# Value loads of the first head pair on two hardware queues, and another order for batch 1's attention

## The chip, the cores and the metric

The kernel runs on one core of a Trainium2 chip. The metric is the device time of one execution in microseconds (us), the median of three runs. The core has five engines that run side by side, each with its own list of instructions in order: TensorE (PE, matrix products; its weight loads appear as PEld), VectorE (DVE), ScalarE (ACT), GpSimd (POOL) and SyncE (SP). Sixteen DMA engines move data between HBM and the on-chip memory. A transfer is issued from SP or ACT (the hardware queues) or from POOL (the software queue, the one that here casts f32 to bf16 on the way).

## The reference

```python
# q, k, v: (8 batches, 8 heads, 1024 positions, 64), f32; E, F: (64, 1024)
k_proj = np.einsum('ks,bhsd->bhkd', E, k)
v_proj = np.einsum('ks,bhsd->bhkd', F, v)
scores = scale * np.matmul(q, k_proj.transpose(0, 1, 3, 2))
attn = softmax(scores)                       # with + 1e-09 in the denominator
x = np.matmul(attn, v_proj)                  # -> (8192 tokens, 512)
...
h = x @ w_in                                 # (512, 2048)
g = h * np.clip(h + 3.0, 0.0, 6.0) / 6.0
out = g @ w_out                              # (2048, 512) -> (8192, 512)
```

The softmax is written out in the reference; it is shortened here to its name.

## The kernel before

The work goes by batch. A batch has 1024 tokens in two blocks of 512 (t = 0, 1). For each block the second half of the program, the two large products, runs 16 groups of `w_in` (a group `fo` gives 128 of the 2048 columns: four 128x512 matmuls over the four parts `ko` of the model's width, L424, then a Relu on ACT, L429, and a product on DVE, L430) and 4 groups of `w_out` (16 matmuls each, L444, then a copy to `o_sb`, L458, and a store from SP, L459). The `w_out` groups of one block are put between the `w_in` groups of the next.

The attention of a batch is worked out ahead and put between these groups. `Attention.project` (L181, 16 matmuls) reduces keys and values with E and F; `keys_out` and `values_out` copy the results on DVE; `turn` transposes the keys with a DMA, and issues later batches' loads on POOL. Heads are taken in four pairs (index j, head pairs 2j and 2j+1). For pair j, `scores` (L209) makes two banks, `exps` (L218) turns them into `aT` on ACT, `sums` and `values` (both L227) make two banks each, `log` and `inverse` (L159, L163) give 1/sum as exp(-ln) on ACT, and `scaled` (L246) writes `xT[:, j]` on DVE, which the `w_in` groups of the next batch read at `ko` = j. The on-chip accumulators are 8 banks, four in the pool `mm` and four in `at`.

Order on every engine is the order of the program text (`manual_schedule`); nothing reorders it. Generators let one function's matmuls be interrupted by others': `second_group` yields after every four of its 16 matmuls.

Batch 0 and batch 1 have their own code:

- At the start, SP loads E and ACT loads F into `ef_f32`. POOL issues, in this order, k and half of q for the pairs 0 to 3, v for the pairs 0 to 3 (L101, `load_pair`), seven pieces of `w_in`, the other half of q, `w_out`, and batch 1's k, v and q. POOL has eight semaphores for its loads, so that each load's issue waits for the landing of the eighth before it. `First.first_block` runs batch 0's first block pair by pair: `keys` (L296), `queries` (L324), `scores`, `keys_transposed`, and then `vals(j)` (L312) for the four pairs between `sums` and `products`. The `vals` of pair 3 is its last reduction.
- `two_groups` runs the first two `w_in` groups of a block together, `ko` by `ko`, so that the last part of `xT` is wanted later. It is used at the head of batch 0's two blocks, and (L545 to L548) at the head of the first block of batches 1 and 2.
- Batch 1's attention: after the group `fo` = 7 of batch 0's second block comes `project`, with `turn` and the two `values_out` in the gaps behind `fo` = 8, 9 and 10. Its four `visit` calls come in the four `w_out` groups of that block, each after the group's first four matmuls: visit 0 makes the scores of three pairs (six banks), visit 1 sums and values of pair 0 and scores of pair 3, visit 2 sums and values of pair 1 and sums of pair 2, visit 3 values of pair 2, sums and values of pair 3. Banks of both pools are used.
- Batches 2 to 7 use the same four visits, in later places. Batch 2's last visit comes directly ahead of batch 2's first `w_in` group; the others have a block in between.

Of the kernel before, what the change touches and what calls it, by code (L numbers as in the profile page):

```python
# [8 lines left out]
f32 = mybir.dt.float32  # L9
# [6 lines left out]
def kernel(  # L16
# [11 lines left out]
    nc = tc.nc  # L28
# [5 lines left out]
    P = 128  # L34
    SO = S // P
    KO = d_model // P
    FO = d_ff // P
    TOK = 512
    NB = S // TOK
    SB = SO // NB  # L40
# [17 lines left out]
    rpool = ctx.enter_context(tc.tile_pool(name="r", bufs=4))  # L58
# [13 lines left out]
    ef_f32 = consts.tile([P, S], f32, name="ef_f32")  # L72
    nc.sync.dma_start(out=ef_f32[:KP], in_=E)
    nc.scalar.dma_start(out=ef_f32[KP:], in_=F)
    nc.scalar.preload_act_table_set("natural_log_exp_and_others")
    ones = consts.tile([P, TOK], bf16, name="ones")
    nc.vector.memset(ones, 1.0)  # L77
# [14 lines left out]
    kqv = {0: {n: raw_tile(n) for n in ("k", "q", "v")}}  # L92
# [6 lines left out]
    def load_pair(n, j):  # L99
        hs = slice(2 * j, 2 * j + 2)  # L100
        nc.gpsimd.dma_start(out=kqv[0][n][:, hs], in_=kqv_dram[n][0][:, hs])  # L101

    for j in range(KO):
        load_pair("k", j)
        load_q0(0, slice(2 * j, 2 * j + 2))
        if j == 0:
            make_identity(nc, ident)
    for j in range(KO):
        load_pair("v", j)

    def load_kqv(b, order="qkv"):
        kqv[b] = {}
# [13 lines left out]
    for i in range(SB):  # L126
        c = slice(i * FO // SB, (i + 1) * FO // SB)
# [20 lines left out]
    def q_transposed(b):  # L148

        t = qT_pool.tile([P, KO, 2, TOK], bf16, tag="qT", name="qT")  # L150
        nc.sync.dma_start_transpose(t.rearrange("p j a (m n) -> p (j a m) n", n=P),
                                    kqv[b]["q"].rearrange("p h s d -> p (h s d)"))
        return t
# [14 lines left out]
    class Attention:  # L168
# [82 lines left out]
        def visit(self, n, following, later):  # L251
            if n == 0:
                last = self.scores(2, pmm)
                firsts = [self.scores(j, pat) for j in range(2)]
                for j, tiles in zip((2, 0, 1), (last, *firsts)):
                    self.exps(j, tiles)
                return lambda: None
            if n == 1:
                den, av = self.sums(0, pmm, pmm), self.values(0, pat, pat)
                last = self.scores(3, pat)  # L260
                recs = self.inverses(den)
                self.exps(3, last)
                return lambda: self.scaled(0, av, recs)
            if n == 2:
                den, av = self.sums(1, pmm, pmm), self.values(1, pat, pat)
                more = self.sums(2, pat, pat)
                recs = self.inverses(den)
                self.recs = []
                later += [lambda i=i: self.recs.append(log(more[i])) for i in range(NB)]
                later += [lambda i=i: inverse(self.recs[i]) for i in range(NB)]  # L270
                return lambda: self.scaled(1, av, recs)
            early = self.values(2, pmm, pmm)
            den, av = self.sums(3, pmm, pat), self.values(3, pat, pat)
            if following:
                following.project()
            self.scaled(2, early, self.recs)
            recs = self.inverses(den)
            if following:
                following.keys_out()
                later += [following.turn] + [lambda a=a: following.values_out(a) for a in range(2)]  # L280
            return lambda: self.scaled(3, av, recs)

# [142 lines left out]
    def h_out(h_ps, g, fo):  # L427
        r = rpool.tile([P, TOK], f32, tag="r", name="r")
        nc.scalar.activation(r, h_ps, AF.Relu, bias=0.5, scale=1.0 / 6.0)  # L429
        nc.vector.scalar_tensor_tensor(g[:, fo, :], r, 1.0, h_ps, op0=ALU.min, op1=ALU.mult)  # L430

    def first_group(xT, t, g, fo):
        h_ps = pmm()
        h_part(h_ps, xT, t, fo, range(KO))
        h_out(h_ps, g, fo)
# [5 lines left out]
    def second_group(b, t, g, c, copy=None):  # L441
        o_ps = pmm()
        for fo in range(FO):
            nc.tensor.matmul(o_ps, g[:, fo, c * P:(c + 1) * P], w_out_sb[:, fo, :],  # L444
                             start=(fo == 0), stop=(fo == FO - 1))
            if fo % SB == SB - 1:
                yield
        o_sb = opool.tile([P, d_model], f32, tag="o_sb", name="o_sb")
        o_dst = out_rows(b, t, c)
        if (b, t, c) == (B - 1, NB - 1, SB - 1):  # L450

            half = slice(0, d_model // 2), slice(d_model // 2, d_model)
            nc.vector.tensor_copy(o_sb[:, half[0]], o_ps[:, half[0]])
            nc.scalar.copy(o_sb[:, half[1]], o_ps[:, half[1]])
            nc.sync.dma_start(out=o_dst[:, half[0]], in_=o_sb[:, half[0]])
            nc.scalar.dma_start(out=o_dst[:, half[1]], in_=o_sb[:, half[1]])
            return
        (copy or nc.scalar.copy)(o_sb, o_ps)  # L458
        nc.sync.dma_start(out=o_dst, in_=o_sb)  # L459

    def whole(gen):
        for _ in gen:
            pass
# [13 lines left out]
    g = [g_tile(), g_tile()]  # L477


    def two_groups(xT, t, g, kos, more=lambda: None):  # L480
        tiles = [pmm(), pmm()]
        for i, (fo, part) in enumerate([(fo, part) for part in kos for fo in range(2)]):
            h_part(tiles[fo], xT, t, fo, part)
            if i == 0:
                more()
        for fo in range(2):
            h_out(tiles[fo], g, fo)

    two_groups(xT, 0, g[0], ((0, 1), (2,), (3,)), lambda: next(by_pairs, None))
    for fo in range(2, FO):  # L490
        first_group(xT, 0, g[0], fo)
        if fo >= FO - 2:
            first.queries(1, (0, 1) if fo == FO - 2 else (2, 3))
    behind, later = [], []
    second = Attention(1)
    second.xT = x_next

    def pop():
        if later:
            later.pop(0)()  # L500

    rows = [second_group(0, 0, g[0], c) for c in range(SB)]
    for i in range(SB + 1):
        for c in range(SB - 1):
# [2 lines left out]
            first.second_scores()  # L507
        elif i < 3:
            first.second_values(2 * i - 2)
    two_groups(xT, 1, g[1], ((0, 1), (2, 3)))  # L510
    for fo in range(2, FO):
        first_group(xT, 1, g[1], fo)
        pop()
        if fo == 7:
            second.project()
            second.keys_out()
            later += [second.turn, *(lambda a=a: second.values_out(a) for a in range(2))]
        elif fo == 11:
            whole(rows[3])
    rest = []  # L520
    for c in range(SB):
        for i, _ in enumerate(second_group(0, 1, g[1], c, nc.vector.tensor_copy)):
            pop()
            if i == 0:
                rest.append(second.visit(c, None, later))
            elif i == 2 or c == SB - 1:
                while rest:
                    rest.pop()()
    qT_dma[2] = q_transposed(2)
    xT = x_next  # L530

    second = Attention(2)
    for b in range(1, B):
        if b + 1 < B:
            x_next = second.xT = x_tile()
        third = Attention(b + 2) if b + 2 < B else None
        n = 0
        for t in range(NB):  # L540
            if b == 1 and t == 1:
                qT_dma[3] = q_transposed(3)
            g = g_tile()
            for fo in range(FO):
                if b < 3 and t == 0 and fo < 2:  # L545

                    if fo == 0:
                        two_groups(xT, t, g, ((0, 1, 2), (3,)))  # L548
                else:
                    first_group(xT, t, g, fo)  # L550
                pop()
                if b > 1 and t == 0 and fo == 5 and third:
                    qT_dma[b + 2] = q_transposed(b + 2)
                if b == 1 and t == 0 and fo == 10:
                    second.project()
                    second.keys_out()
                    later += [second.turn, *(lambda a=a: second.values_out(a) for a in range(2))]
                if not behind or fo % SB < SB - 1:
                    continue
                if b + 1 == B or n == 4:  # L560
                    whole(second_group(*behind[0], fo // SB))
                    continue
                rows = second_group(*behind[0], fo // SB, nc.vector.tensor_copy)
                if n < 3:
                    next(rows)
                    next(rows)
                    rest = second.visit(n, third, later)
                    whole(rows)
                else:
                    whole(rows)  # L570
                    rest = second.visit(n, third, later)
                rest()
                n += 1
            behind = [(b, t, g)]
        second, xT = third, x_next
# [32 lines left out]
```

## Time and profile before

| | us |
|---|---|
| median of 3 runs | 510.52 (510.51 to 510.60) |
| the profiled execution, its own time | 510.52 |
| its span from first to last instruction | 508.7 |
| PE busy | 497.5 |
| ACT busy | 274.0 |
| DVE busy | 258.0 |
| POOL busy | 37.9 |

Granted clock of TensorE: 1.000 over the whole span. In the groups of instructions, L444 is busy 231.6 us and L424 229.1 us, 379 ns each; since matmuls overlap in the pipeline, the distance between two starts says more than the duration. In the windows and timelines below, times count from the span's start; "idle before" is the time for which the engine had nothing to do, and the arrow names what ended it.

### The profile page before, as it was taken

What the parts mean: (1) busy time and instruction counts of PE and PEld (TensorE: products, weight loads), DVE (VectorE), ACT (ScalarE), POOL (GpSimd) and SP (SyncE); (2) the same over time, 40 slices, a digit from 0 to 9 for tenths busy, and PEclk for the clock granted to TensorE, in tenths of its full rate; (3) what the DMA queues carried; (4) which work ended last, traced back from release to release, by engine and by line L of the source; (5) the groups of instructions that cost most, each with busy time, mean ns of one, the idle gap of its engine ahead of it and who ended that gap; (6) DMA issues with size and microseconds to landing.
All of it is one profiled execution on the core that took longest, in us unless ns stands there. A gap on an engine that the chain in (4) does not pass through costs nothing.

```text
span 508.7 us, 7106 instructions
## 1 busy us (share of the span) xinstructions
PE 497.5 (98%) x2750; PEld 224.3 (44%) x2802; DVE 258.0 (51%) x401; ACT 274.0 (54%) x493; POOL 37.9 (7%) x57
## 2 busy tenths in 40 slices
PE   8899999999999999999999999999999999999996
PEld 4444444444444444444444444444444444444442
DVE  3572746856755733556444743467444563334420
ACT  3657476567475545664466644674447654444431
POOL 8610020010100200002000020000000000000000
PEclk9999999999999999999999999999999999999999
DMA  9999999599299592516923188411110011101112
GB/s 170 200 205 207 199 155 239 98 170 203 53 191 203 78 220 65 125 42 105 216 63 84 52 147 175 103 51 33 43 41 34 29 43 43 43 24 39 41 51 74
DMA packets 74210, 55.39 MB, mean 109 GB/s; under 512 B 35520, under 2 KB 65984, under 8 KB 74176
## 3 DMA queue, kind: packets, MB, share of 16 engines
q0 software_dynamic: 31952, 29.36, 36.9%
q1 hardware_dynamic: 42000, 25.17, 19.2%
q10 hardware_dynamic: 224, 0.39, 0.3%
q8 instruction: 22, 0.36, 0.3%
q14 instruction: 12, 0.10, 0.1%
HBM read 59.24 MB, written 16.78 MB: 149 GB/s over the span
## 4 chain that ended last, share of the span: by engine, by line
PE 94%; DMA 2%; POOL 2%; issue 1%; DVE 0%; ACT 0%; DVEq 0%; POOLq 0%
PE mm L444 44%; PE mm L424 43%; PE at L181 3%; DMA v<-in_v_dram 2%; PE mm L227 2%; PE at L227 1%; PE at L209 1%; POOL q L97 1%; PE mm L209 1%; POOL k L101 1%; POOL v L101 0%; PE at L344 0%; DVE kp L187 0%; PE at L324 0%; PE at L312 0%
## 5 line engine op out<-in xcount | busy, mean ns | idle before, releaser
L430 DVE SCALAR_TENSOR_TENSOR g<-r,mm 128x512 bf16<-128x512 f32 x256 | 173.9, 687 | 132.3 <-ACT r L429 130.9
L444 PE MATMUL mm<-w_out_sb,g 128*128 128x512 bf16 x997 | 231.6, 379 | 1.8 <-issue 0.6
L424 PE MATMUL mm<-xT,w_in_sb 128*128 128x512 bf16 x999 | 229.1, 379 | 1.8 <-DVE xT L246 0.6
L429 ACT ACTIVATE r<-mm 128x512 f32<-128x512 f32 x256 | 152.6, 599 | 76.1 <-PE mm L424 74.2
L424 PEld LDWEIGHTS <-w_in_sb 128*128 128x128 bf16 x1024 | 99.4, 98 | 122.8 <-issue 4.8
L444 PEld LDWEIGHTS <-g 128*128 128x128 bf16 x1024 | 98.1, 98 | 121.6 <-issue 7.0
L458 ACT COPY o_sb<-mm 128x512 f32<-128x512 f32 x35 | 20.3, 587 | 91.5 <-PE mm L444 91.5
L458 DVE COPY o_sb<-mm 128x512 f32<-128x512 f32 x28 | 19.4, 692 | 67.0 <-PE mm L444 67.0
L159 ACT ACTIVATE rec<-mm 128x512 f32<-128x512 f32 x39 | 21.8, 595 | 37.0 <-PE mm L227 20.1
L163 ACT ACTIVATE rec<-rec 128x512 f32<-128x512 f32 x60 | 35.6, 638 | 0.0
L246 DVE TENSOR_TENSOR xT<-at,rec 128x512 bf16<-128x512 f32 x42 | 26.9, 680 | 5.1 <-ACT rec L163 5.1
L218 ACT ACTIVATE aT<-at 128x512 bf16<-128x512 f32 x42 | 22.1, 616 | 0.0
L199 POOL COPY mark<-kT 1x1 bf16<-1x1 bf16 x5 | 0.9, 178 | 209.0 <-DMA kT<-kp 209.0
L159 ACT ACTIVATE rec<-at 128x512 f32<-128x512 f32 x25 | 14.6, 599 | 2.3 <-PE at L344 2.3
L181 PE MATMUL at<-k,e_t 128*64 128x512 bf16 x56 | 13.4, 382 | 0.0
L181 PE MATMUL at<-v,f_t 128*64 128x512 bf16 x56 | 13.4, 382 | 0.0
L218 ACT ACTIVATE aT<-mm 128x512 bf16<-128x512 f32 x14 | 7.6, 594 | 9.5 <-PE mm L209 9.5
L187 DVE CAST kp<-at 64x512 bf16<-64x512 f32 x14 | 9.0, 678 | 4.9 <-PE at L181 4.9
L190 DVE CAST vp<-at 64x512 bf16<-64x512 f32 x14 | 9.7, 694 | 0.4
L246 DVE TENSOR_TENSOR xT<-mm,rec 128x512 bf16<-128x512 f32 x14 | 9.0, 682 | 0.6 <-PE mm L227 0.6
L84 PE MATMUL mm<-ones 128*128 128x512 bf16 x18 | 7.4, 548 | 1.5 <-DVE ones L77 1.5
L181 PEld LDWEIGHTS <-e_t 128*64 128x64 bf16 x56 | 5.6, 109 | 7.2 <-PE at L227 2.1
(62 smaller groups left out, 142.0 us busy)
## 6 DMA issues: line engine op xcount, KB each, us to landing
out_dram<-o_sb SPq DMA_DIRECT2D x63, 256.0 KB, 2.0
k<-in_k_dram POOLq DMA_DIRECT2D x7, 1024.0 KB, 15.4
v<-in_v_dram POOLq DMA_DIRECT2D x7, 1024.0 KB, 20.5
q<-in_q_dram POOLq DMA_DIRECT2D x7, 1024.0 KB, 10.5
w_out_sb<-in_moe_w_out_dram POOLq DMA_DIRECT2D x4, 512.0 KB, 16.8
k<-in_k_dram POOLq DMA_DIRECT2D x4, 256.0 KB, 5.6
v<-in_v_dram POOLq DMA_DIRECT2D x4, 256.0 KB, 7.8
w_in_sb<-in_moe_w_in_dram POOLq DMA_DIRECT2D x2, 512.0 KB, 11.7
```

Source lines behind the costliest of these rows:

```text
L159: nc.scalar.activation(ln, den, AF.Ln)
L163: nc.scalar.activation(ln, ln, AF.Exp, scale=-1.0)
L181: nc.tensor.matmul(ps[e * KP:(e + 1) * KP], ef_t[e][:, so, :], kqv[self.b]["kv"[e]][:, :, so, :], start=(so == 0), stop=(so == SO - 1))
L209: nc.tensor.matmul(tiles[r][t * KP:(t + 1) * KP, a * HT:(a + 1) * HT], self.kT[r * D:(r + 1) * D, 2 * j + a, :], qT[r * D:(r + 1) * D, j, ...
L218: nc.scalar.activation(self.aT[j][:, r].rearrange("p a n -> p (a n)"), tiles[r], AF.Exp, scale=scale)
L227: nc.tensor.matmul(tiles[t][c:c + D].rearrange("p (r n) -> p r n", r=2), stationary(r, 2 * j + a), self.aT[j][r:r + KP, :, a, :], start=Tr ...
L246: nc.vector.tensor_mul(self.xT[:, j, t, :], av[t], recs[t])
L424: nc.tensor.matmul(h_ps, w_in_sb[:, ko, fo * P:(fo + 1) * P], xT[:, ko, t, :], start=(ko == 0), stop=(ko == KO - 1))
L429: nc.scalar.activation(r, h_ps, AF.Relu, bias=0.5, scale=1.0 / 6.0)
L430: nc.vector.scalar_tensor_tensor(g[:, fo, :], r, 1.0, h_ps, op0=ALU.min, op1=ALU.mult)
L444: nc.tensor.matmul(o_ps, g[:, fo, c * P:(c + 1) * P], w_out_sb[:, fo, :], start=(fo == 0), stop=(fo == FO - 1))
L458: (copy or nc.scalar.copy)(o_sb, o_ps)
```

## The change

Three things are done. (1) The values of pair 0 (heads 0 and 1) are no longer loaded by POOL's queue with a cast; each head is loaded as f32 by a hardware queue, head 0 from SP behind E and head 1 from ACT behind F, into two buffers of the pool `r`, and cast to bf16 by POOL behind the issue of the third remaining value pair, ahead of the issues of `w_in`. (2) Batch 1's attention is no longer made of visits. A plan of steps is drawn one step at a time: behind `fo` = 7, 8, 9 and 10, and then after every four matmuls of the four `w_out` groups. It gives six insertions in the `w_out` groups: scores of pairs 0 and 1, scores of pairs 2 and 3, and sums with values for each of the four pairs, all in the four banks `at`. (3) `two_groups` is no longer used at the head of batches 1 and 2.

```diff
+    v_f32 = []
+    for a, queue in enumerate((nc.sync, nc.scalar)):
+        v_f32.append(rpool.tile([P, TOK], f32, tag="r", name="r").rearrange("p (s d) -> p s d", s=SO))
+        queue.dma_start(out=v_f32[a], in_=kqv_dram["v"][0][:, a])
...
-    for j in range(KO):
+    for j in range(1, KO):
         load_pair("v", j)
+    for a in range(2):
+        nc.gpsimd.tensor_copy(kqv[0]["v"][:, a], v_f32[a])
...
+        def two_scores(self, j):
+            tiles = [self.scores(i, pat) for i in (j, j + 1)]
+            for i in range(2):
+                self.exps(j + i, tiles[i])
+
+        def normalised(self, j):
+            den, av = self.sums(j, pat, pat), self.values(j, pat, pat)
+            recs = self.inverses(den)
+            yield
+            self.scaled(j, av, recs)
+            yield
+            yield
...
+        def steps(self, plan):
+            for wait, part, *args in plan:
+                for _ in range(wait):
+                    yield
+                yield from getattr(self, part)(*args) or ()
...
+    PLAN = ((0, "project"), (0, "keys_out"), (1, "turn"), (0, "values_out", 0), (2, "values_out", 1),
+            (1, "two_scores", 0), (2, "two_scores", 2), (2, "normalised", 0),
+            (0, "normalised", 1), (0, "normalised", 2), (0, "normalised", 3))
...
-    second = Attention(1)
-    second.xT = x_next
...
+    ahead = Attention(1)
+    ahead.xT = x_next
+    ahead = ahead.steps(PLAN)
...
     for fo in range(2, FO):
         first_group(xT, 1, g[1], fo)
-        pop()
-        if fo == 7:
-            second.project()
-            second.keys_out()
-            later += [second.turn, *(lambda a=a: second.values_out(a) for a in range(2))]
+        if fo in (7, 8, 9, 10):
+            next(ahead)
         elif fo == 11:
             whole(rows[3])
-    rest = []
     for c in range(SB):
-        for i, _ in enumerate(second_group(0, 1, g[1], c, nc.vector.tensor_copy)):
-            pop()
-            if i == 0:
-                rest.append(second.visit(c, None, later))
-            elif i == 2 or c == SB - 1:
-                while rest:
-                    rest.pop()()
+        for _ in second_group(0, 1, g[1], c, nc.vector.tensor_copy):
+            next(ahead, None)
     qT_dma[2] = q_transposed(2)
+    whole(ahead)
...
             for fo in range(FO):
-                if b < 3 and t == 0 and fo < 2:
-
-                    if fo == 0:
-                        two_groups(xT, t, g, ((0, 1, 2), (3,)))
-                else:
-                    first_group(xT, t, g, fo)
-                pop()
+                first_group(xT, t, g, fo)
+                if later:
+                    later.pop(0)()
```

The remaining lines of the diff change the arguments of `two_groups` at batch 0's blocks, without another effect.

More of the change, by code (lines that the diff above doesn't have):

```diff
@@ L477, with two_groups @@
     g = [g_tile(), g_tile()]
-    def two_groups(xT, t, g, kos, more=lambda: None):
+    def two_groups(t, kos, more):
         tiles = [pmm(), pmm()]
@@ L486, in two_groups @@
         for fo in range(2):
-            h_out(tiles[fo], g, fo)
-    two_groups(xT, 0, g[0], ((0, 1), (2,), (3,)), lambda: next(by_pairs, None))
+            h_out(tiles[fo], g[t], fo)
+    two_groups(0, ((0, 1), (2,), (3,)), lambda: next(by_pairs, None))
     for fo in range(2, FO):
@@ L493 @@
             first.queries(1, (0, 1) if fo == FO - 2 else (2, 3))
-    behind, later = [], []
-    second = Attention(1)
-    second.xT = x_next
-    def pop():
-        if later:
-            later.pop(0)()
+    ahead = Attention(1)
+    ahead.xT = x_next
+    ahead = ahead.steps(PLAN)
     rows = [second_group(0, 0, g[0], c) for c in range(SB)]
@@ L509 @@
             first.second_values(2 * i - 2)
-    two_groups(xT, 1, g[1], ((0, 1), (2, 3)))
+    two_groups(1, ((0, 1), (2, 3)), lambda: None)
     for fo in range(2, FO):
         first_group(xT, 1, g[1], fo)
-        pop()
-        if fo == 7:
-            second.project()
-            second.keys_out()
-            later += [second.turn, *(lambda a=a: second.values_out(a) for a in range(2))]
+        if fo in (7, 8, 9, 10):
+            next(ahead)
         elif fo == 11:
             whole(rows[3])
-    rest = []
     for c in range(SB):
-        for i, _ in enumerate(second_group(0, 1, g[1], c, nc.vector.tensor_copy)):
-            pop()
-            if i == 0:
-                rest.append(second.visit(c, None, later))
-            elif i == 2 or c == SB - 1:
-                while rest:
-                    rest.pop()()
+        for _ in second_group(0, 1, g[1], c, nc.vector.tensor_copy):
+            next(ahead, None)
     qT_dma[2] = q_transposed(2)
+    whole(ahead)
     xT = x_next
+    behind, later = [], []
     second = Attention(2)
```

## The prediction

> **What bounds the kernel now.** I read the page first, then the chain of waits in order of time, then TensorE's timeline in the three places that the change touches.
>
> ```profile
> span 508.7 us, 7106 instructions
> PE 497.5 (98%) x2750; PEld 224.3 (44%) x2802; DVE 258.0 (51%) x401; ACT 274.0 (54%) x493; POOL 37.9 (7%) x57
> DMA  9999999599299592516923188411110011101112
> ```
>
> TensorE (PE) is the bound. Busy time alone would not prove it, so I measured the distance between starts: a 128x512 matmul follows the one before it after 0.216 us, and from 21 us on nearly every start keeps that distance. A gain can therefore come only from the first 20 us, or from the few places where the distance is longer; a loss can come from anywhere that adds such a place.
>
> The chain of waits for the start and for the beginning of block 2:
>
> ```profile
> 7.59 2.13 POOL v L101 x3
> 9.72 9.92 DMA v<-in_v_dram
> 19.64 0.05 issue
> 19.69 0.62 PE at L312 x8
> ...
> 131.36 1.89 PE at L181 x16
> 133.25 0.02 issue
> 133.28 1.28 DVE kp L187 x2
> 134.56 0.61 DVE xT L246
> 135.17 0.04 issue
> 135.21 2.32 PE mm L424 x10
> ```
>
> The first four lines say that PE starts its long run when the last value pair (v3) has landed; the rest that PE waits at 135.21 for the last product of batch 2's attention.
>
> TensorE's timeline, the start and the middle (start, us, operation):
>
> ```profile
> 11.15 0.63 PE L296 MATMUL at<-k,e_t 128*64 128x128 bf16 x8
> ...
> 18.75 0.40 PE L344 MATMUL at<-aT,vp 64*64 64x512 bf16 x2
> 19.69 0.62 PE L312 MATMUL at<-v,f_t 128*128 128x128 bf16 x8 [0.54 <-DMA v<-in_v_dram]
> ...
> 41.28 0.41 PE L344 MATMUL at<-aT,ones 64*64 64x512 bf16 x4
> 41.52 0.39 PE L344 MATMUL at<-aT,vp 64*64 64x512 bf16 x4
> 41.84 2.76 PE L444 MATMUL mm<-w_out_sb,g 128*128 128x512 bf16 x12
> ...
> 76.54 0.41 PE L227 MATMUL mm<-aT,ones 64*64 64x512 bf16 x4
> 76.78 0.39 PE L227 MATMUL at<-aT,vp 64*64 64x512 bf16 x4
> 77.00 0.39 PE L227 MATMUL at<-aT,ones 64*64 64x512 bf16 x4
> 77.31 3.63 PE L444 MATMUL mm<-w_out_sb,g 128*128 128x512 bf16 x16
> ```
>
> In the trace's semaphore updates the loads of the start land at (us) k0 6.52, q0 7.20, k1 8.52, q1 9.16, k2 10.62, q2 11.30, k3 12.59, q3 13.27, v0 14.54, v1 15.82, v2 17.10, v3 19.64. A pair takes 1.28 us of all 16 DMA engines, one after the other. v3 is the exception: 15 of its 16 parts are there at 18.40, and the last waits for an engine that moved a 16 KB packet of instructions from 17.61 for 0.95 us. Those packets come once in about 256 PE instructions (this one after 125 matmuls and 130 weight loads), so they move with PE's progress.
>
> **Part 1, the value loads.** Removed: POOL's issue of v0 (0.72 us, the first of those from 7.59 on). Added: an f32 load of 256 KB behind E on SP and behind F on ACT, and two casts on POOL behind v3's issue.
>
> Price of the loads. The pair is 512 KB of f32 in both forms, 256 runs of 2 KB. The trace has no f32 load of 2 KB runs. Nearest rows: E's and F's 4 KB packets took 0.159 us when undisturbed, 0.08 us per 2 KB; and at 51 to 55 us, where 2 KB stores run beside a casting load, 382 store packets and 412 load packets passed in 4 us, where the load alone passes about 205 per us. So a 2 KB packet costs what a casting packet costs, and the pair again costs 1.28 us. Bounds: nothing, if the hardware queues bring bandwidth of their own; 2.56 us, if a 2 KB packet takes the 0.159 us of a 4 KB one. I take 1.28, by the nearer row. The engines have no hole to put it in: E's and F's packets fill them from 2.1 to about 4.9 us, and k0's begin at 3.92. So it goes in ahead of k1 at the latest: k1 to q3 land 1.28 us later, v1 to v3 when they did.
>
> What is late next. The eight L296 matmuls of keys pair 2 ran at 11.15, 0.53 after k2 landed. With k2 at 10.62 + 1.28 = 11.90 they start at 11.95: 0.80 later. From there the block has no slack: sums, ACT's Ln and Exp (0.60 and 0.63, in a row from 12.16 on), queries, scores, values and DVE's products follow each other. So the last operation ahead of v3's matmuls, values for pair 2 at 18.75, comes at 19.55. The group behind such a pair of matmuls starts 0.34 after it (17.20 to 17.54, 18.09 to 18.43), so v3's matmuls could start at 19.09 before and at 19.89 now. The instruction packet moves with PE to about 18.4, when v3's slowest ordinary part (18.40 landed, some 0.4 earlier moved) is through; v3 then lands at 18.40 and no longer decides. Cost: 19.89 - 19.69 = **+0.20 us**. By the bounds: -0.60 (19.09) for nothing; for 2.56 us, 2.08 + 19.09 - 19.69 = +1.48.
>
> One rule of the Trainium skill speaks against this part: "DMA: Bandwidth & Descriptors", section "Issuing engines are not separate DMA queues", has loads from SP, ACT and POOL share the same 16 engines, so that another queue saves the issue alone. By the rule the part gives +0.20; without it, -0.60. The trace's 51 to 55 us agrees with the rule.
>
> The casts. POOL has no 128x512 cast. Its 128x128 memset (0.23) and select (0.29), times four, give 0.92 and 1.16; DVE's same cast took 0.65. Bounds 0.65 and 1.16 each; I take 1.0, 2.0 together. v3's issue waits for k1's slot (8.52 + 1.28 = 9.80) and ends at 10.5, so the casts end at 12.5, and v0's matmuls come at 15.70 + 0.80. Cover 4 us. Behind the casts stand all w_in issues: the first goes from 10.91 to 12.5, but v3 holds the engines until 18.0, so its data moves when it did. Without that cover the casts would cost w_in their 2 us. fo 2 and fo 8 have the least slack on w_in: 0.36 (21.95 landed, 22.36 used) and 0.34 (27.20, 27.54); 0.20 later only widens it. ACT's table load starts 0.58 later, at 1.93, and is used at 5.77 first. Two buffers of r are taken by the f32 tiles until 12.5; ACT wants them from 23 us. All at nothing.
>
> **Part 2, batch 1's attention in six insertions in place of four.** The same 64 small matmuls enter the same w_out groups. From the last L444 start ahead to the first behind, less one matmul: the eight of 41.28 cost 41.84 - 40.97 - 0.22 = 0.65; the sixteen scores of 38.02 also 38.58 - 37.71 - 0.22 = 0.65; the twelve of 76.54 cost 77.31 - 76.23 - 0.22 = 0.86. The four visits were 0.87 + 0.88 + 0.86 + 0.87 = 3.48. Six insertions of 0.65 are 3.92. Cost **+0.43 us**: four matmuls cost 0.21, the rest is 0.22 for each change of shape and back.
>
> Waits there: only four banks ("at") are used now. Counted from each insertion's first matmul with the rows of 38 to 48 us (Ln starts after 0.44, Exp after 1.42, products after 2.08, end at 2.77 and 3.37; exps end at 1.05, 1.54, 2.04, 2.53): the second scores come at 2.38 and 2.62 and want banks free at 1.54 and 2.53; values 0 at 5.1 want a bank free at 4.91; the next values come at 3.48 and want 2.77, at 3.58 want 3.37; block 1's fourth matmul comes at 0.56 + 8 x 0.216 + 3 x 0.216 = 2.93 and wants the product of 2.77. Each just fits, by 0.1 to 0.2. I take 0; bounds 0 and 0.6, if each of six is late by 0.1. DVE's value copy moves from fo 9 to fo 8; PE reuses the bank of fo 9 only after 16 matmuls of rows 3 (3.45 us), which covers its 0.69. PE reads the queries' transposes at 67.87, landed 66.90; the order of SP and POOL behind it is unchanged.
>
> **Part 3, the paired groups at the head of blocks 1 and 2 go.** Block 1: covered as just shown (2.93 against 2.77); cost 0, or 0.16 less cover. Block 2: before, six of eight matmuls stood ahead of the wait that ends at 135.21 and two behind. Now three stand ahead and five behind; the wait's end is DVE's, after two kp copies, and does not move. Cost 3 x 0.216 = **+0.65 us**, nothing hides it. Blocks 3 to 7 never had the pairing.
>
> **Sum.** The profiled execution took 510.52 (span 508.7, 1.8 around it), which is also the median of the three runs. 510.52 + 0.20 + 0.43 + 0.65 = 511.80.
>
> **Rivals.** (a) Not slower by more than can be told: the f32 loads cost the casting queue nothing. One mechanism, decided at the start: if k2 lands by 10.7, keys keep 11.15 and v3's matmuls move to 19.09. For it: from 3 to 4 us the packets carry 326 KB, against 205 of a casting load's halved bytes later; against it: 51 to 55 us. Price -0.60: 510.52 + 1.08 - 0.60 = 511.0, +0.1%. (b) v3 is late anyway: if keys slip by less than 0.2, the instruction packet meets v3 again and PE starts at 19.69 as before: 511.6. (c) F's packets are delayed too, or 2 KB packets cost 0.159: e_t or k2 decides, +1.48: 513.1. (d) The six insertions wait for banks: +0.6: 512.4. (e) That the change does not do what it says, bringing v0 sooner: v0 landed at 14.54 and was used at 15.70, so its coming sooner is worth nothing in any case; this is in the forecast and has no time of its own.
>
> **How the numbers follow.** Forecast 0.45 (own range 511.6 to 512.1), a 0.17, b 0.14, c 0.10, d 0.11, and 0.03 for something faster that no row shows. The range 510.9 to 512.7 holds all but the upper part of c. A measurement of this kernel tells about 0.2% (1.02 us) from no change: slower means above 511.54. Forecast, c, d and about half of b are: 0.73. Same, a and the rest of b: 0.24. Faster 0.03: after 21 us PE has only losses to take, and the start offers at most 0.60.
>
> **What would show it.** Keys pair 2 at 11.9 and k2's landing at the same time; v3 landed near 18.4 and no DMA wait ahead of the last L312, which starts near 19.9; six insertions of 0.65 between block 1's w_out matmuls; at block 2 a wait of about 1.25 in place of 0.60. The forecast is wrong if k2 lands near 10.6, if v3's matmuls start before 19.3 or after 20.3, or if a wait on DVE or ACT appears at the insertions.

## The result, and the profile after

The changed kernel took 511.94 us in the median of 6 runs (511.64 to 512.38), beside 510.52 (510.40 to 510.60) for the kernel before in as many: a ratio of 1.0028, with a 95% interval of 1.0015 to 1.0041. It is slower, by 1.42 us in the medians. The profiled execution took 511.77 with a span of 510.0.

The head of the page of the changed kernel (span; busy time; DMA engines in 40 slices):

```profile
span 510.0 us, 7113 instructions
PE 497.5 (98%) x2750; PEld 224.5 (44%) x2802; DVE 257.9 (51%) x401; ACT 274.4 (54%) x493; POOL 38.3 (8%) x58
DMA  9999989599199493515914188421110111101112
```

Nothing here says that the kernel is slower but the span: PE's busy time is the same to a tenth. The loss is idle time and changes of shape, and these have to be read where they lie. TensorE's timeline of the changed kernel (start, us, operation, idle time before it and what ended it):

```profile
12.05 0.63 PE L329 MATMUL at<-k,e_t 128*64 128x128 bf16 x8 [0.17 <-DMA k<-in_k_dram]
...
19.98 0.62 PE L345 MATMUL at<-v,f_t 128*128 128x128 bf16 x8
20.71 0.38 PE L457 MATMUL mm<-xT,w_in_sb 128*128 128x512 bf16 x1
...
76.26 0.41 PE L234 MATMUL at<-aT,ones 64*64 64x512 bf16 x4
76.50 0.39 PE L234 MATMUL at<-aT,vp 64*64 64x512 bf16 x4
76.82 2.76 PE L477 MATMUL mm<-w_out_sb,g 128*128 128x512 bf16 x12
79.52 0.41 PE L234 MATMUL at<-aT,ones 64*64 64x512 bf16 x4
79.75 0.39 PE L234 MATMUL at<-aT,vp 64*64 64x512 bf16 x4
...
85.06 1.24 PE L457 MATMUL mm<-xT,w_in_sb 128*128 128x512 bf16 x5
...
136.02 2.97 PE L457 MATMUL mm<-xT,w_in_sb 128*128 128x512 bf16 x13 [1.25 <-DVE xT L253]
138.83 1.89 PE L477 MATMUL mm<-w_out_sb,g 128*128 128x512 bf16 x8
```

In the order of time: the wait for v3 ahead of the last value reduction (L345 now) is gone, and a wait for k stands ahead of the keys instead. From 76.26 to 79.52 a pair's sums and values and the twelve matmuls behind them take 3.26 us; there is no wait at any of the six insertions. At block 2 the wait for DVE's product is 1.25 where it was 0.60; the row of the kernel before is

```profile
135.21 2.32 PE L424 MATMUL mm<-xT,w_in_sb 128*128 128x512 bf16 x10 [0.60 <-DVE xT L246]
```

The chain of waits of the changed kernel names the start's new bound, a key pair's transfer where a value pair's stood before:

```profile
4.72 7.28 DMA k<-in_k_dram
12.00 0.04 issue
12.05 0.63 PE at L329 x8
```

Where the time went is best seen by setting the same event of two traces beside each other. The table does this for all profiled kernels against the profile of before: how much later the projection of batch 1 starts (54.69 before), what is added from there to batch 2's projection (93.84 before; block 1), and from there to batch 4's projection (165.18 before; block 2). From there to the last product on DVE no difference changes by more than 0.02 us; the closing copies and stores after it make up for as much as 0.25. The medians are those of the runs, with those of the kernel before beside them.

| kernel | start | block 1 | block 2 | median | before | ratio, 95% interval |
|---|---|---|---|---|---|---|
| changed | +0.35 | +0.47 | +0.51 | 511.94 | 510.52 | 1.0015 to 1.0041 |
| changed, second profile | +0.94 | +0.46 | +0.51 | 512.06 | 510.63 | 1.0018 to 1.0039 |
| loads alone | +1.42 | 0 | 0 | 510.78 | 510.60 | 1.0000 to 1.0017 |
| plan alone | +0.21 | +0.46 | 0 | 511.09 | 510.60 | 1.0000 to 1.0018 |
| no paired groups | -0.16 | 0 | +0.51 | 510.97 | 510.60 | 1.0001 to 1.0018 |
| changed, pair back at block 2 | +0.70 | +0.47 | -0.01 | 511.25 | 510.60 | 1.0002 to 1.0020 |
| two pairs as f32 | +1.56 | 0 | 0 | 512.01 | 510.56 | 1.0016 to 1.0036 |
| 7 warming matmuls | +0.43 | 0 | 0 | 510.81 | 510.56 | 0.9996 to 1.0013 |
| three groups at block 2 | +0.72 | 0 | +0.56 | 511.15 | 510.56 | 1.0000 to 1.0018 |
| sums and values split | +0.88 | +1.38 | +0.51 | 512.91 | 510.56 | 1.0035 to 1.0062 |
| three copies on ACT | +0.32 | 0 | -0.34 | 510.30 | 510.63 | 0.9984 to 1.0002 |
| other order of copies | +0.19 | 0 | -0.38 | 510.01 | 510.42 | 0.9983 to 1.0001 |

The columns of blocks 1 and 2 repeat to 0.02 us, whatever else was changed. The start does not: it differs by 0.9 us among the six profiles with the loads of before at the start (-0.16 to 0.72, that of before at 0) and by 1.1 us among the five with one f32 pair (0.35 to 1.42). The whole time of the kernel before differs by 1.7 us among 33 runs on a later chip (510.08 to 511.76); no trace shows in which part. A single profile is no measure of the start.

The three parts alone lie 0.18, 0.49 and 0.37 us over before in the medians, 1.04 together, where the whole change has 1.42. Each of the three intervals is about 0.4 us wide to either side, so this is no contradiction, but the division of the loss rests on the columns of blocks 1 and 2 and not on these medians.

### The profile page after: what moved, and what is told of

The parts are those of the page before. It is cut to its first block, busy times and chain, and to the rows that moved or that the text cites. A ratio compares the mean times of both kernels' runs of the same rounds, so it can differ in the third digit from the quotient of the medians.

```text
span 510.0 us, 7113 instructions
## 1 busy us (share of the span) xinstructions
PE 497.5 (98%) x2750; PEld 224.5 (44%) x2802; DVE 257.9 (51%) x401; ACT 274.4 (54%) x493; POOL 38.3 (8%) x58
## 4 chain that ended last, share of the span: by engine, by line
PE 95%; DMA 1%; issue 1%; POOL 1%; DVE 1%; ACT 0%; DVEq 0%; POOLq 0%
PE mm L477 43%; PE mm L457 43%; PE at L188 3%; PE at L234 1%; PE mm L234 1%; DMA k<-in_k_dram 1%; PE at L216 1%; PE at L377 0%; PE at L345 0%; PE mm L216 0%; POOL q L102 0%; DVE kp L194 0%; PE at L357 0%; PE mm L377 0%; POOL k L106 0%
## 5 line engine op out<-in xcount | busy, mean ns | idle before, releaser
L166 ACT ACTIVATE rec<-mm 128x512 f32<-128x512 f32 x34 | 19.0, 595 | 34.3 <-PE mm L234 17.6
L253 DVE TENSOR_TENSOR xT<-at,rec 128x512 bf16<-128x512 f32 x44 | 28.1, 680 | 7.0 <-ACT rec L170 7.0
L166 ACT ACTIVATE rec<-at 128x512 f32<-128x512 f32 x30 | 17.3, 598 | 6.0 <-PE at L234 3.7
L225 ACT ACTIVATE aT<-mm 128x512 bf16<-128x512 f32 x12 | 6.5, 594 | 8.9 <-PE mm L216 8.9
L234 PE MATMUL at<-aT,vp 64*64 64x512 bf16 x88 | 8.5, 376 | 0.0
```

Of the source, the lines that this page charges most:

```text
L166: nc.scalar.activation(ln, den, AF.Ln)
L225: nc.scalar.activation(self.aT[j][:, r].rearrange("p a n -> p (a n)"), tiles[r], AF.Exp, scale=scale)
L234: nc.tensor.matmul(tiles[t][c:c + D].rearrange("p (r n) -> p r n", r=2), stationary(r, 2 * j + a), self.aT[j][r:r + KP, :, a, :], start=Tr ...
L253: nc.vector.tensor_mul(self.xT[:, j, t, :], av[t], recs[t])
```

## The experiments

**The loads alone.** The kernel before, with the first part of the change.

```diff
+        queue.dma_start(out=v_f32[a], in_=kqv_dram["v"][0][:, a])
...
-    for j in range(KO):
+    for j in range(1, KO):
         load_pair("v", j)
+    for a in range(2):
+        nc.gpsimd.tensor_copy(kqv[0]["v"][:, a], v_f32[a])
```

> The kernel before with part 1 alone (value pair 0 as f32 on the hardware queues, cast by GpSimd). Theory: the f32 pair takes 1.28 us of the DMA engines ahead of k1, keys pair 2 starts near 12.0, v3 lands near 18.4 and its matmuls start near 20.0: time 510.52 + 0.35 = 510.87, ratio 1.0007. Rival, the loads are free and the 0.35 us of the start came with other parts: keys pair 2 stays at 11.15, v3's matmuls at 19.1, time 509.9 to 510.5.

The median is 0.18 us over that of before, the mean of the 11 runs 0.36 (511.02 against 510.66), the interval of the ratio begins at 1.0000. The theory said 0.35; no change at all lies at the interval's edge, so the times of this run alone do not show the loss. The rival's 509.9 to 510.5 lies below the interval, and its keys at 11.15 were not met. The profiled execution is one of the longest of its row (511.83; one part of k0 landed 0.9 late), which makes the mechanism plain. TensorE's timeline of this kernel:

```profile
9.24 0.61 PE L303 MATMUL at<-k,e_t 128*64 128x128 bf16 x8 [1.66 <-DMA k<-in_k_dram]
...
11.27 0.61 PE L303 MATMUL at<-k,e_t 128*64 128x128 bf16 x8 [0.27 <-DMA k<-in_k_dram]
...
13.18 0.63 PE L303 MATMUL at<-k,e_t 128*64 128x128 bf16 x8 [0.18 <-DMA k<-in_k_dram]
...
15.09 0.61 PE L303 MATMUL at<-k,e_t 128*64 128x128 bf16 x8 [0.23 <-DMA k<-in_k_dram]
```

All four key reductions wait for a k. Before the change the third ran 0.53 after its k had landed; this slack is spent, and a late k now delays TensorE nearly one for one: in the five profiles with one f32 pair k2 landed at 12.00, 12.28, 12.42, 12.47 and 13.13, and the start took 0.35, 0.70, 0.88, 0.94 and 1.42 more.

**Two pairs as f32.** Value pairs 0 and 1 on the hardware queues, two heads each.

```diff
+    for a in range(4):
+        queue = (nc.sync, nc.scalar)[a % 2]
...
+        queue.dma_start(out=v_f32[a], in_=kqv_dram["v"][0][:, a])
...
-    for j in range(KO):
+    for j in range(2, KO):
         load_pair("v", j)
+    for a in range(4):
+        nc.gpsimd.tensor_copy(kqv[0]["v"][:, a], v_f32[a])
```

> The kernel before with two value pairs (0 and 1) as f32 on the hardware queues, cast by GpSimd, in place of one. Theory (each f32 pair takes 1.28 us of the same 16 DMA engines ahead of k1, and keys now wait for k): k2 lands near 13.2 to 13.4, each keys group starts 0.05 after its k, v3's matmuls start near 21.2: about 1.3 us over the kernel with one such pair, 510.78 + 1.3 = 512.1. Rival 1, the hardware queues bring bandwidth: k2 within 0.3 of the 12.0 seen with one pair, time near 510.8. Rival 2, v3 decides and not the keys: v3's matmuls start 0.05 after v3's landing, time 510.6 to 510.9.

The median is 512.01 where 512.1 was forecast. In the semaphore updates k2 lands at 13.27 and k3 at 15.24, 1.27 and 1.32 behind the changed kernel's. Its timeline:

```profile
13.31 0.63 PE L304 MATMUL at<-k,e_t 128*64 128x128 bf16 x8
...
15.28 0.61 PE L304 MATMUL at<-k,e_t 128*64 128x128 bf16 x8 [0.28 <-DMA k<-in_k_dram]
...
21.24 0.62 PE L320 MATMUL at<-v,f_t 128*128 128x128 bf16 x8
```

The keys start 0.04 after their k. v3 had landed at 18.50, 2.7 us before its matmuls at 21.24, so it decides nothing. Both rivals fall: the f32 loads take the shared engines' time.

**The plan alone.** The six insertions, with the paired groups kept at blocks 1 and 2.

```diff
-                rest.append(second.visit(c, None, later))
...
+        for _ in second_group(0, 1, g[1], c, nc.vector.tensor_copy):
+            next(ahead, None)
```

> The kernel before with part 2 alone (six insertions by the plan, the paired groups at the heads of blocks 1 and 2 kept). Theory: six insertions of 0.65 us in place of 3.48 us in four, no waits: 510.52 + 0.45 = 510.97, ratio 1.0009. Rival, the plan itself is free or better and only loses with a shifted start (waits for banks that an earlier start would not meet): within 0.1 us of 510.52.

Block 1 takes 0.46 more in the profile, the medians differ by 0.49 (the interval begins at 1.0000). The loss needs no shifted start, and the rival falls.

**Sums and values split.** The changed kernel; the same 64 small matmuls of block 1 in ten insertions.

```diff
-            den, av = self.sums(j, pat, pat), self.values(j, pat, pat)
+            den = self.sums(j, pat, pat)
             recs = self.inverses(den)
             yield
+            av = self.values(j, pat, pat)
             self.scaled(j, av, recs)
```

> The changed kernel with the sums and the values of each pair of batch 1 in insertions of their own, four matmuls apart: ten insertions in place of six, the same matmuls. Theory: 0.22 us for each change of shape and back, 4 x 0.22 = 0.88: 511.9 + 0.9 = 512.8. Rival, the 0.45 us of the change was waiting for banks and products, which four more insertions do not add to: 511.9 to 512.1.

Block 1 takes 1.38 more than before, 0.92 over the changed kernel's: 0.23 for each of four more insertions. Its timeline:

```profile
77.02 0.41 PE L234 MATMUL at<-aT,ones 64*64 64x512 bf16 x4
77.36 1.04 PE L478 MATMUL mm<-w_out_sb,g 128*128 128x512 bf16 x4
78.33 0.41 PE L234 MATMUL at<-aT,vp 64*64 64x512 bf16 x4
78.67 1.90 PE L478 MATMUL mm<-w_out_sb,g 128*128 128x512 bf16 x8
```

Four matmuls from 77.02 and four from 77.36 would follow at their usual distance in 0.21 and 0.86; here they take 0.34 and 0.97. No wait stands in the rows, only the changes of shape: the price belongs to the insertion.

**No paired groups, and the pair put back.** The kernel before without the pairing at the heads of blocks 1 and 2, and the changed kernel with it at block 2.

```diff
-                if b < 3 and t == 0 and fo < 2:
+                if False:
```

```diff
-                first_group(xT, t, g, fo)
+                if b == 2 and t == 0 and fo < 2:
+                    if fo == 0:
...
+                else:
+                    first_group(xT, t, g, fo)
```

> The kernel before without the paired groups at the heads of blocks 1 and 2. Theory: nothing at block 1 that PE's later products do not hide by 0.1 to 0.2 us, at block 2 three matmuls more behind the wait for DVE's product, 0.65, of which 0.14 comes back at the scores that follow, where one bank comes late before: 510.52 + 0.51 = 511.03, ratio 1.0010; with visits kept, block 1's fourth matmul may wait for visit 3's product too, up to 0.6 more. Rival, the loss at block 2 belongs to the plan's shift: no change.

> The changed kernel with the paired groups put back at the head of block 2 alone. Theory: the 0.51 us of block 2 come back, and the scores' late bank returns with them: 511.94 - 0.5 = 511.4, ratio to before 1.0018. Rival, the wait at block 2 is bound elsewhere and pairing gives nothing: 511.9.

Without the pairing, block 1 is unchanged and block 2 takes 0.51 more; with it put back, block 2 is as before, and the median falls to 511.25 (forecast 511.4). The rows of the two kernels, the unpaired one first:

```profile
135.04 2.97 PE L424 MATMUL mm<-xT,w_in_sb 128*128 128x512 bf16 x13 [1.25 <-DVE xT L246]
```

```profile
136.37 2.32 PE L457 MATMUL mm<-xT,w_in_sb 128*128 128x512 bf16 x10 [0.60 <-DVE xT L253]
...
140.59 0.74 PE L216 MATMUL at<-qT,kT 64*64 64x256 bf16 x16
```

The wait is 1.25 without and 0.60 with: the 0.65 of three matmuls. With the pair, the sixteen scores that follow take 0.74 in place of the 0.61 of other such groups; the tenth of them starts 0.05 after DVE's second value copy ends (140.87), whose bank is wanted. Without it PE comes later and does not wait: 0.65 - 0.14 = 0.51.

**Seven warming matmuls.** The kernel before, with five fewer of the matmuls on ones that open the program.

```diff
-    busy(12)
+    busy(7)
```

> The kernel before with 7 in place of 12 warming matmuls at the start, which are no part of the result; that takes 10 of TensorE's instructions away ahead of the keys. Theory: the 16 KB packet of instructions comes 10 PE instructions later, after the reduction of pair 2 and not in it, at about 18.1; v3's last part is no longer held up and lands near 18.4, its matmuls start at 19.1 to 19.4 if the prologue keeps its pace, and w_in's first pieces take the delay: 510.5 - 0.3 = 510.2. Rival, the packet's time is not tied to PE's place: at 17.6, v3 at 19.6, time as before; and TensorE may be slower behind the shorter warming, then later than before.

The packet of instructions came at 18.69, in place of 17.61; v3 landed at 18.37, its 15th part at 18.30, in place of 19.64 and 18.40. So v3 is not held up when the packet comes after it. The gain did not come. TensorE's timeline, the kernel before first:

```profile
7.77 0.63 PE L296 MATMUL at<-k,e_t 128*64 128x128 bf16 x8
...
9.46 0.63 PE L296 MATMUL at<-k,e_t 128*64 128x128 bf16 x8
...
17.54 0.62 PE L312 MATMUL at<-v,f_t 128*128 128x128 bf16 x8
```

```profile
7.87 1.06 PE L296 MATMUL at<-k,e_t 128*64 128x128 bf16 x8
...
10.50 0.63 PE L296 MATMUL at<-k,e_t 128*64 128x128 bf16 x8
...
18.57 0.62 PE L312 MATMUL at<-v,f_t 128*128 128x128 bf16 x8
...
20.12 0.62 PE L312 MATMUL at<-v,f_t 128*128 128x128 bf16 x8
```

The first eight key matmuls take 1.06 in place of 0.63, though the granted clock is 1.0 there; the prologue loses 1.04 by its second keys (10.50 against 9.46) and keeps that to v3's matmuls at 20.12. Time 510.81, no change that can be told. The packet was not moved in the way that was forecast. It was to come ten instructions later, behind the reduction of pair 2; it came 0.12 behind the start of that reduction (18.57), much as before (0.07 behind 17.54). It was later because the whole prologue was later, and why taking ten instructions away did not shift its place is open. Of the rival, the first half (a packet that does not go with PE) falls, and the second half (a slower TensorE) is what happened.

**Three groups at block 2.** The kernel before; its wait of 0.60 at block 2 should be covered by three more matmuls.

```diff
-                if b < 3 and t == 0 and fo < 2:
+                wide = 3 if b == 2 else 2
+                if b < 3 and t == 0 and fo < wide:
...
-                        two_groups(xT, t, g, ((0, 1, 2), (3,)))
+                        tiles = [pmm() for _ in range(wide)]
+                        for part in ((0, 1, 2), (3,)):
+                            for n2 in range(wide):
+                                h_part(tiles[n2], xT, t, n2, part)
+                        for n2 in range(wide):
+                            if b == 2:
+                                pop()
+                            h_out(tiles[n2], g, n2)
```

> The kernel before with the first three w_in groups of block 2 taken together instead of two, and the value copies put between their DVE products. Theory: block 2's wait for DVE's last product (0.60) is covered by three more matmuls, 0.65: 510.5 - 0.5 = 510.0, ratio 0.9990. Rival, the wait comes back at the scores that follow, because a bank there is free only after DVE's second value copy: no change.

A miss. The edit also puts the value copies between the groups' products. The wait at the first groups goes, and comes back larger at the scores:

```profile
139.13 0.69 DVE L190 CAST vp<-at 64x512 bf16<-64x512 f32 x1
...
139.86 1.28 DVE L430 SCALAR_TENSOR_TENSOR g<-r,mm 128x512 bf16<-128x512 f32 x2
140.60 0.41 PE L209 MATMUL mm<-qT,kT 64*64 64x256 bf16 x7 [0.78 <-DVE g L430]
```

The scores need a bank of `mm` that the third group's product frees, and this stands behind both value copies on DVE. Block 2 takes 0.56 more. DVE is the bound there, and PE's work put ahead of a wait only moves it.

**Copies moved off DVE.** If so, DVE's copies are what to move. First three of batch 3's four projection copies to ACT, then both value copies to ACT with the second key copy between the halves of the last product.

```diff
-            if following:
+            if following and self.b == 2:
...
+                nc.vector.tensor_copy(following.kp[:, :, 0, :], heads)
+                nc.scalar.copy(following.kp[:, :, 1, :], heads)
+                for a in range(2):
+                    nc.scalar.copy(following.vp[a * KP:(a + 1) * KP],
+                                   following.ps[KP:].rearrange("p (h d) -> p h d", d=D))
```

```diff
+            if following and self.b == 2:
...
+                nc.vector.tensor_copy(following.kp[:, :, 0, :], heads)
+                for a in range(2):
+                    nc.scalar.copy(following.vp[a * KP:(a + 1) * KP],
+                                   following.ps[KP:].rearrange("p (h d) -> p h d", d=D))
...
+                    nc.vector.tensor_mul(self.xT[:, 3, 0, :], av[0], recs[0])
+                    nc.vector.tensor_copy(following.kp[:, :, 1, :], heads)
+                    nc.vector.tensor_mul(self.xT[:, 3, 1, :], av[1], recs[1])
```

> The kernel before, with three of the four copies of batch 3's projection (second key copy, both value copies) moved from DVE to ACT, at batch 2's last visit alone. Theory: at block 2 DVE is the bound: two key copies stand ahead of the product that TensorE waits for, two value copies between the products of the next groups. With one key copy ahead the wait of 0.60 goes, and the 0.14 at the scores with it: 510.6 - 0.7 = 509.9, ratio 0.9986. Rival, ACT's own products (Relu of the first groups) come late behind the copies, 1.8 us of them: no change or up to 0.5 slower.

> The kernel before; at batch 2's last visit ACT makes both value copies of batch 3's projection, and DVE makes first key copy, first half of the last product, second key copy, second half. Theory: the product that TensorE waits for at block 2 comes 0.64 earlier, so that of the wait of 0.60 at most 0.2 is left, and the bank that the scores wait 0.14 for is free in time; ACT's copies end before the first Relu is wanted, unlike with three copies on ACT: 510.6 - 0.55 = 510.05, ratio 0.9989. Rival, the key transpose that starts later (behind the second key copy) comes too late for batch 3's scores at 139: no gain.

Block 2 takes 0.34 and 0.38 less than before, where 0.7 and 0.55 were expected; the medians are 0.33 and 0.41 under that of before, and both intervals still reach 1. These are the only versions whose medians lie under that of the kernel before; that they beat it is likely and not shown. The second one's rows name what is left:

```profile
134.18 1.18 ACT L282 CAST vp<-at 64x512 bf16<-64x512 f32 x2 [0.69 <-DVE kp L280]
...
135.38 0.68 DVE L287 CAST kp<-at 64x512 bf16<-64x512 f32 x1 [0.64 <-ACT vp L282]
...
137.31 1.89 PE L458 MATMUL mm<-w_out_sb,g 128*128 128x512 bf16 x8 [0.20 <-DVE g L444]
```

ACT's copies wait for DVE's first key copy, and DVE's second waits for them, all readers of the one projection bank. They come one after another on two engines (why readers of one bank wait for each other is not shown), and PE keeps a wait of 0.20 at the next `w_out` group.

**The changed kernel again.**

> The changed kernel again, as it stands, on the chip of these runs and with another profile. Theory: from the first value matmul on the same as in the first profile (0.45 more in block 1, 0.51 more in block 2), and only the start differs, by as much as k2's landing does: total 511.6 to 512.4. Rival, the spread of 0.7 us between its runs comes from later stages: the differences in block 1 or 2 change.

The median is 512.06. Blocks 1 and 2 add 0.46 and 0.51 as before, and the start 0.94 where the first profile has 0.35, with k2 landed at 12.47 and not at 12.00. The theory holds: between these two profiles the difference lies in the start alone.

## Why the prediction was right

The forecast was 511.80, slower; 511.94 was measured. The mechanisms held, but the sum came closer than its terms: the start was forecast 0.15 or more too small and the paired groups 0.14 too large, and that the two offset is luck. Point by point:

- *The f32 pair displaces k by 1.28.* k2 landed at 12.00 (forecast 11.90), its keys started at 12.05 (11.95), the value matmuls at 19.98 (19.89). The f32 packets of 2 KB took 0.096 us in the median, the casting load's 0.098: the price taken from the stores' row was right, and two pairs doubled it. The counts in that row (382 and 412) have 32 and 11 packets of 4 bytes in them; without these it is 350 and 401, which gives the same price. The pair did not go in between k0 and k1 but ran beside k0 too: k0 landed at 8.19 in place of 6.52, and the first keys waited for it, from 7.77 to 8.24.
- *v3 no longer decides.* It landed at 18.45 (18.40); the packet of instructions came at 18.41 (about 18.4) and held up `w_in`'s first piece instead, which landed at 20.44 where it had been 19.93.
- *The start's size, +0.20, was small.* It was 0.35 in the profile: 0.29 at v3's matmuls, where k2's landing 0.10 later than forecast accounts for the 0.09 over the forecast, and 0.06 more to the projection. The prediction read the start as one number from one profile, and it is a spread. In the kernels with one f32 pair, the medians less the columns of blocks 1 and 2 leave 0.18 to 0.46 for it, an estimate. Whether the change makes the spread of the runs wider is not shown: 0.74 against 0.20 in the first runs, but 1.21 against 1.00 in the second ones, and with two pairs, where the keys wait too, 0.38 against 1.24.
- *The casts at nothing.* Two took 1.18 us together (2.0 estimated), from 11.00 to 12.18, 4.4 us before the value reduction at 16.59. The slack of fo 2 on `w_in` is 0.41 by the prediction's two times (21.95 and 22.36) and not 0.36; nothing hung on it.
- *Six insertions, +0.43.* 0.47 in the profile, 0.46 alone; 0.23 for each further one (0.22 by the rows).
- *No wait at the four banks.* None was there; rival (d) falls.
- *Paired groups, +0.65 at block 2 and 0 at block 1.* The wait grew by 0.65, and block 1 lost nothing. "Nothing hides it" was wrong: 0.14 comes back at the scores, so that the term is 0.51. 0.35 + 0.47 + 0.51 = 1.33 up to the last copies, and 1.25 between the two executions' times.
- *Rivals.* (a), free loads, falls with the two pairs. In (b), a late v3, the packet came when the forecast had it and missed v3. (c), a start of +1.48, was met in no median of one pair, though one profile of the loads alone had 1.42.

## What to carry to other kernels

A transfer on another queue is not a transfer for nothing where all queues share engines that are full: ask which transfer it passes and who waits for that one, before asking who waits for its own. Work inserted in TensorE's stream has a price for each change of shape and back (0.22 us here), so fewer and larger insertions are better where the banks allow it. Work put ahead of a wait covers it only if the engine that ends the wait is not the bound of the next stage too; there, take work off that engine.

## What the runs showed of the hardware

With 7 in place of 12 warming matmuls at the start, eight key matmuls took 1.06 us in place of 0.63 while the granted clock was shown as 1.0; here the clock in the profile did not say how fast TensorE ran. And a 16 KB packet of instructions, which in the kernel before comes 22 times, once in about 250 of TensorE's recorded instructions, takes one DMA engine for 0.95 us: it made one part of one load 1.24 us later than the other fifteen. In the thirteen profiles the first such packet came between 17.15 and 20.05 us, in twelve of them from 0.02 before to 0.50 behind the start of the third value reduction and in one 0.75 ahead of it, so that TensorE's progress decides which load it meets.
